# A written-out order of issue replaced by a list scheduler, weights converted in PSUM pieces, and epsilon as a ninth column of a sum

## The chip, the cores and the metric

The kernel runs on one core of one Trainium2 chip. The metric is the device time of one execution in microseconds (us) on that core. Everything is float32 at the borders, except the weights, which arrive as float64 words. The profile shows one execution; its times run from the first to the last instruction (the span).

## The reference

Four batches of four heads attend linearly over 1088 tokens with head size 32; the heads' outputs stand side by side as 128 columns and go through a gated feed-forward layer (here: the ffn) with 1024 inner columns.

```python
def phi(x):
    a = np.einsum('rd,bhsd->bhsr', S1, x)
    b = np.einsum('rd,bhsd->bhsr', S2, x)
    return np.einsum('bhsi,bhsj->bhsij', a, b).reshape(*x.shape[:-1], r * r)
q_p, k_p = (phi(q), phi(k))
kv = np.einsum('bhsf,bhsd->bhfd', k_p, v)
z = np.sum(k_p, axis=2)
num = np.einsum('bhsf,bhfd->bhsd', q_p, kv)
den = np.einsum('bhsf,bhf->bhs', q_p, z)[..., None] + 1e-06
...
h = np.maximum(x @ w_in, 0.0)
for k in range(3):
    conv_out += conv_w[k][None, None, :] * hp[:, k:k + S, :]
gate = 1.0 / (1.0 + np.exp(-conv_out))
return (h * gate @ w_out).astype(np.float32)
```

## The kernel before

**Attention.** Tokens go in chunks of 128, three chunks to a group, three groups to a batch. On the k side of a group, `k_ab` multiplies the chunks with S1 and S2 on TensorE (L389), `k_take` copies the result out of PSUM on ScalarE (L393), `k_phi` makes the outer products (L370, on VectorE or on GpSimd, by the table `KPHI`), and `k_kv` adds them up against v in one bank of PSUM (L425). `k_z`, `k_zmask`, `k_wz` and `k_wq` make the sum z of the batch and fold it with S2 (L405 to L416); `k_kvmask`, `k_kvt` and `k_kvtake` bring the batch's kv into place (L436 to L444). On the q side of a group `q_ab` multiplies (L452), `q_take` copies (L456), `q_ac` and `q_sum` make the denominator (L460, L464), `q_eps` adds epsilon to it (L467, 12 elements a partition), `q_rec` and `q_div` divide (L470, L473), `q_phi` makes the outer products (L370), two `q_t` transpose them (L488), two `q_ttake` copy (L492), `q_x` multiplies with kv (L500), and `q_hi` and `q_lo` split the result x into a rounded part and a rest (L514, L517).

**The ffn.** The tokens of all batches stand in one row of columns, cut into nine segments (382 columns, seven times 510, 404). A unit is one segment with one of eight blocks of 128 inner columns, 72 units in all. A unit is `f_in`, three matmuls in an accumulation (L571 to L573); `f_relu` and `f_mid` on ScalarE (L578, L582); two taps of the convolution on VectorE (L586); `f_gate` on ScalarE (L592); `f_mul` on GpSimd (L597, the last unit's on VectorE); and `f_out`, one float32 matmul into the segment's sum (L602), which the trace shows as two instructions. After eight units the sum is copied and stored (L608, L613). The first segment needs x of one group of tokens only.

**Weights.** A float64 weight becomes a float32 in seven or eight steps: `low` on ScalarE (L289), two bit fields and a clamp on VectorE (L292 to L294), a multiply-add `f` (L295), `power` on ScalarE (L302), `sign` on VectorE (L305), `value` on GpSimd (L311); w_in is split further into a rounded part on ScalarE (L340) and a rest on GpSimd (L343). Each matrix is done in two halves of 512 columns, with all working tiles in SBUF. One packed array of 216 columns (S1, S2, the convolution's weights) goes first, wholly on VectorE.

**Order.** Each engine takes its instructions in program order. Up to a key that stands for the first unit's beginning, the order on four engines is that of keys written out by hand (`FIRST`, `WEIGHTS`); later only the ffn on TensorE and ScalarE is held to such keys, and the rest goes where the framework puts it. Tiles come from pools that rotate; TensorE's results have 4 banks of PSUM for units, 1 for the segment's sum, 3 for the attention. Loads are started on SyncE's queue, and two of them (half of w_in, batch 1's k) on ScalarE's. Eight idle matmuls stand before the first real one, and one more later (L272).

Of the kernel before, what the change touches and what calls it, by code (L numbers as in the profile page):

```python
# [78 lines left out]
STEPS = {
    "k_ab": (0.05, 1.01),  # L80
    "k_take": (0.4, 1),
    "k_phi": (0.65, 1),
    "k_kv": (3.25, 1),
    "k_z": (3.32, 0),
    "k_zmask": (3.47, 0),
    "k_wz": (4.04, 0),
    "k_wq": (4.38, 0),
    "k_kvmask": (5.98, 0),
    "k_kvt": (7.25, 0),
    "k_kvtake": (7.4, 0),  # L90
    "q_ab": (0.2, 0),
    "q_take": (0.4, 0),
    "q_ac": (0.57, 0),
    "q_sum": (0.91, 0),
    "q_eps": (1.28, 0),
    "q_rec": (1.82, 0),
    "q_div": (2.24, 0),
    "q_phi": (3.06, 0),
    "q_t": (5.1, 0),
    "q_ttake": (5.81, 0),  # L100
    "q_x": (6.21, 0),
    "q_hi": (6.4, 0),
    "q_lo": (7.41, 0),
}
# [1 line left out]
FREE = 0.1
# steps of a unit of the ffn after its own key; the last units' products go to VectorE
LATE = 1
LAGS = (0, 0.28, 0.5, 0.6, 0.66, 2.35, 3.5, 5.05, 5.19)
L_IN, L_RELU, L_MID, L_TAPA, L_TAPB, L_GATE, L_MUL, L_OUT, L_STORE = LAGS  # L110
# batch -> (key of its k side, stretch), keys of its groups' q sides
KSIDE = [None, (-2.55, 1.0), (5.56, 1.5), (18.12, 1.78)]
QSIDE = [[None, -2.98, -0.34], [2.08, 8.05, 9.86], [15.15, 31.42, 37.29], [38.03, 45.98, 50.18]]
# the first batch and the weights, on a scale of their own: two steps to a key, the first unit stands at T0
T0 = 18.2
WQ_S = 6.84
FIRST = {
    "k_ab": (7.1, 0.24),
    "k_take": (7.8, 0.48),
# [562 lines left out]
```

## Time and profile before

| | |
|---|---|
| median of 3 runs | 185.1 us (185.1 to 186.12) |
| span of the profiled execution | 183.1 us |
| the profiled execution's own time | not recorded apart from the runs; two of the three took 185.1 us, 2.0 us more than the span |
| TensorE, VectorE, ScalarE, GpSimd busy | 172.1, 153.1, 142.6, 122.8 us |
| mean granted clock of TensorE | 0.972 |
| bytes read, written | 9.15 MB, 2.23 MB |

In the profile PE is TensorE's matmuls, PEld its loads of weights, DVE is VectorE, ACT ScalarE, POOL GpSimd, SP SyncE. The rows of the timeline give start and duration; durations of neighbours on one engine overlap a little, since each starts before the one ahead has drained, so that the cost of one is read from start to start. "x12" after a float32 matmul counts two instructions for each in the program. PEclk is the granted clock of TensorE as a share of the full one.

### The profile page before, as it was taken

The page shows a single profiled execution, that of the slowest core. Times are in us where ns is not written, and L with a number is a line of the kernel's source. Part 1 is how long each engine was busy: PE and PEld are TensorE (multiplying, and loading weights), DVE is VectorE, ACT ScalarE, POOL GpSimd, SP SyncE. Part 2 cuts the span into 40 slices and gives each one's busy share as a digit, 9 for nine tenths or more (in the row PEclk, how much of TensorE's full clock was granted, in tenths as well). Part 3 has the DMA queues.
Part 4 walks back from the last instruction along what each step waited for, and adds up shares of the span by engine and source line. Part 5 has one row for each costly group of instructions (what it writes and reads, how often), then busy time and mean ns, then how long its engine had stood idle before and what let it go on. Part 6 is the DMA issues. An engine that isn't in the chain of part 4 may idle for free.

```text
span 183.1 us, 2698 instructions
## 1 busy us (share of the span) xinstructions
PE 172.1 (94%) x870; PEld 112.9 (62%) x870; DVE 153.1 (84%) x270; ACT 142.6 (78%) x297; POOL 122.8 (67%) x111
## 2 busy tenths in 40 slices
PE   7696888999999999999999999999999999999992
PEld 6584756767777565756666566664656565566640
DVE  2769999997788849977669998898989997999981
ACT  3235455499975798897778999899899999999960
POOL 1135568598985535998556697478569795779760
PEclk9999657999999999999999999999999999999999
DMA  5999992000000100010001001000100100010101
GB/s 141 378 356 343 354 380 53 0 4 2 0 0 4 43 0 2 0 61 0 0 0 57 5 0 57 2 0 0 57 4 0 54 3 0 2 57 0 58 3 45
DMA packets 9005, 11.54 MB, mean 63 GB/s; under 512 B 544, under 2 KB 7712, under 8 KB 8992
## 3 DMA queue, kind: packets, MB, share of 16 engines
q1 hardware_dynamic: 8704, 10.30, 17.1%
q10 hardware_dynamic: 288, 1.08, 1.6%
q8 instruction: 7, 0.11, 0.3%
q14 instruction: 6, 0.05, 0.1%
HBM read 9.15 MB, written 2.23 MB: 62 GB/s over the span
## 4 chain that ended last, share of the span: by engine, by line
PE 57%; POOL 13%; DVE 10%; issue 7%; ACT 4%; DMA 4%; SPq 3%; POOLq 1%; DVEq 0%; ACTq 0%
PE o L602 19%; POOL g L597 13%; PE a L571 7%; PE a L572 6%; PE a L573 6%; DMA w_in_raw<-in_w_in 4%; PE t L425 4%; PE t L500 4%; PE t L452 4%; PE t L488 4%; PE t L389 2%; DVE f L295 2%; ACT s L592 2%; SPq L233 2%; DVE a L586 1%
## 5 line engine op out<-in xcount | busy, mean ns | idle before, releaser
L586 DVE SCALAR_TENSOR_TENSOR a<-h,pws,a 128x510 f32<-128x510 f32 (+2 forms) x144 | 102.4, 722 | 16.8 <-ACT a L582 14.5
L597 POOL TENSOR_TENSOR g<-h,s 128x510 f32<-128x510 f32 (+2 forms) x71 | 86.5, 1223 | 36.5 <-ACT s L592 34.3
L602 PE MATMUL o<-g,w_out_sb 128*128 128x510 f32 (+2 forms) x144 | 70.3, 572 | 0.9 <-DVE o L608 0.5
L578 ACT ACTIVATE h<-a 128x512 f32<-128x512 f32 (+2 forms) x72 | 42.6, 592 | 13.2 <-PE a L573 13.1
L582 ACT ACTIVATE a<-h,pws 128x510 f32<-128x510 f32 (+2 forms) x72 | 49.8, 692 | 0.0
L571 PE MATMUL a<-xhi,whi 128*128 128x512 f32 (+2 forms) x72 | 45.7, 635 | 0.0
L592 ACT ACTIVATE s<-a 128x510 f32<-128x510 f32 (+2 forms) x72 | 42.5, 591 | 3.2 <-DVE a L586 2.8
L602 PEld LDWEIGHTS o<-g,w_out_sb 128*128 128x128 f32 x144 | 26.5, 189 | 8.8 <-POOL g L597 1.8
L572 PE MATMUL a<-xhi,wlo 128*128 128x512 f32 (+2 forms) x72 | 27.9, 388 | 0.0
L573 PE MATMUL a<-xlo,whi 128*128 128x512 f32 (+2 forms) x72 | 27.9, 387 | 0.0
L571 PEld LDWEIGHTS a<-xhi,whi 128*128 128x128 f32 x72 | 13.8, 192 | 13.6 <-issue 7.3
L572 PEld LDWEIGHTS a<-xhi,wlo 128*128 128x128 f32 x72 | 13.8, 192 | 9.3 <-issue 8.7
L370 POOL TENSOR_TENSOR kp<-kab 128x768 f32<-128x768 f32 x9 | 13.8, 1533 | 5.8 <-ACT kab L393 5.7
L573 PEld LDWEIGHTS a<-xlo,whi 128*128 128x128 f32 x72 | 13.7, 190 | 2.5
L370 POOL TENSOR_TENSOR qp<-qm,qab 128x768 f32<-128x768 f32 x9 | 13.6, 1512 | 1.7 <-DVE qm L473 1.5
L389 PEld LDWEIGHTS t<-pws,kt 128*128 128x128 f32 x72 | 10.3, 214 | 6.5 <-issue 3.1
L389 PE MATMUL t<-pws,kt 128*128 128x64 f32 x72 | 11.0, 300 | 1.7 <-DVE m L293 1.4
L452 PEld LDWEIGHTS t<-wq,qt 128*128 128x128 f32 x72 | 10.1, 202 | 3.4 <-issue 1.2
L488 PEld LDWEIGHTS t<-pks,qp 128*128 128x128 f32 x72 | 8.8, 148 | 5.4 <-issue 2.6
L425 PE MATMUL t<-kp,vt 128*64 128x128 f32 x144 | 11.5, 288 | 0.3 <-DMA vt<-in_v 0.3
L488 PE MATMUL t<-pks,qp 128*128 128x128 f32 x72 | 10.9, 288 | 0.8 <-DVE qp L370 0.8
L492 ACT COPY qt<-t 128x384 f32<-128x384 f32 x24 | 10.8, 505 | 1.0 <-PE t L488 0.9
(65 smaller groups left out, 150.5 us busy)
## 6 DMA issues: line engine op xcount, KB each, us to landing
qt<-in_qT SPq DMA_DIRECT2D x4, 544.0 KB, 8.2
vt<-in_v SPq DMA_DIRECT2D x4, 512.0 KB, 9.3
kt<-in_kT SPq DMA_DIRECT2D x3, 544.0 KB, 9.0
w_out_raw<-in_w_out SPq DMA_DIRECT2D x2, 512.0 KB, 8.5
out<-o SPq DMA_DIRECT2D x4, 255.0 KB, 2.2
kt<-in_kT ACTq DMA_DIRECT2D x1, 544.0 KB, 7.5
...
```

The source lines that it names most:

```text
L370: e.tensor_tensor(out=out.rearrange("p c (h i j) -> p (c h) i j", i=R, j=R), in0=a.unsqueeze(3).broadcast_to([P, n, R, R]), in1=b.unsqueez ...
L389: nc.tensor.matmul(pv[:, :, j, :], kt[:, b, c * P : (c + 1) * P], sab, start=True, stop=True)
L488: nc.tensor.transpose(ps[:, j * P : (j + 1) * P], st["qp", g][:, j, P * pr : P * (pr + 1)], ident)
L571: nc.tensor.matmul(a[:, : n + 2], whi[:, w], xhi[:, x], start=True, stop=False)
L572: nc.tensor.matmul(a[:, : n + 2], wlo[:, w], xhi[:, x], start=False, stop=False)
L573: nc.tensor.matmul(a[:, : n + 2], whi[:, w], xlo[:, x], start=False, stop=True)
L578: nc.scalar.activation(h[:, : n + 2], a[:, : n + 2], AF.Relu)
L582: nc.scalar.activation(st["a"][:, :n], h, AF.Copy, scale=cw[:, f, 1:2])
L586: nc.vector.scalar_tensor_tensor(out=a[:, :n], in0=h[:, k : n + k], scalar=cw[:, f, k : k + 1], in1=a[:, :n], op0=ALU.mult, op1=ALU.add)
L592: nc.scalar.activation(s[:, :n], st["a"][:, :n], AF.Sigmoid)
L597: e.tensor_tensor(out=gt[:, :n], in0=st["h"][:, 1 : n + 1], in1=st["s"][:, :n], op=ALU.mult)
L602: nc.tensor.matmul(acc[g][:, :n], w_out_sb[:, f * P : (f + 1) * P], st["g"][:, :n], start=f == 0, stop=f == NF - 1)
```

## The change

All keys and stretches go. A function `graph` lists every step with its engine, an assumed cost, the steps that it needs, and the buffers that it takes and frees; `schedule` runs through them as a list scheduler: of the engines' next possible steps it takes the one that can begin first, and among those of an engine that can begin within 30 ns of each other the one with the lowest due time. It assumes that VectorE and GpSimd exclude each other in steps marked `lock` or `twice`. All four engines follow the resulting order from beginning to end, and every tile stands in the buffer that the scheduler gave it.

Beside the order:

- The weights of w_in and w_out are converted in pieces of 256 columns, eight in all, and the two integer fields stand in a bank of PSUM of the attention's three, not in SBUF. `sign` takes its field from PSUM and writes to a third SBUF tile.
- The packed small weights are split in two arrays, S1 and S2 for the attention (64 columns) and the rest (152 columns), converted one after the other.
- `q_eps` is gone. The tile that `q_ac` writes has a ninth column, set to epsilon once at the start in three buffers, and `q_sum` adds nine elements.
- All loads are on SyncE's queue, in another order; v comes padded with zeros and laid out so that a batch is one transfer (two before, and a memset of the padding), w_out in one row for each partition.
- Of the 24 groups of outer products five change engine: batch 0's third k group and batch 2's third q group go from VectorE to GpSimd, batch 1's first two q groups and batch 3's third k group go from GpSimd to VectorE. VectorE then has seven of them (six before).
- The idle matmuls come from the scheduler: where TensorE's planned gap before 22 us is over 300 ns, one for each 430 ns.

```diff
-CVT = 512
+CVT = 256
-LOADS = "s i0 k0 c v0 q0 i1 v1 o0 o1 q1 k1 k2 v2 q2 q3 k3 v3"
-EARLY = "i0 k1"
-WARM = 8
+    "loads": "s t k0 c v0 i0 q0 o0 o1 k1 i1 v2 k3 v1 q2 k2 v3 q1 q3",
+    "kphi": ["DPP", "PPP", "PPP", "DPD"],
+    "qphi": ["DPP", "DDD", "PPP", "PPP"],
+    "fills": 22000.0,
+POOLS = {"u": 4, "o": 1, "t": 3, "h": 6, "s": 3, "g": 6, "f": 3, "w": 3, "kab": 6, "kp": 4, "qs": 3, "qp": 2, "qt": 4, "kv": 2}
+FILL = 430.0
...
+            if able:
+                soonest = min(t for t, _, _ in able)
+                _, t, _, name = min((key, t, str(name), name) for t, name, key in able if t <= soonest + 30)
+                if best is None or t < best[0]:
+                    best = t, e, name
+        t, e, name = best
+        (_, occ, lat, shared), _, alloc, _ = events[name]
+        for b in alloc:
+            slot[b] = heapq.heappop(pools[kind_of[b]])[1]
+        if e == "PE" and t < cfg["fills"]:
+            fills[name] = max(0, int((t - now[e] - 300) / FILL))
...
+                em = bank(("cv", *key), "t", "em").bitcast(I32)
+                st["e"], st["m"] = em[:, :n], em[:, n : 2 * n]
...
+            if not small:
+                st["w"] = buffer(("w", *key), "w", [P, n], "w", I32)
             nc.vector.scalar_tensor_tensor(
-                out=st["e"], in0=hi, scalar=-(2**31), in1=st["e"], op0=ALU.bitwise_and, op1=ALU.bitwise_or
+                out=st["w"], in0=hi, scalar=-(2**31), in1=st["e"], op0=ALU.bitwise_and, op1=ALU.bitwise_or
             )
...
+        for m in qms:
+            nc.vector.memset(m[:, :, R:], EPS)
...
-        def q_eps(g):
-            nc.vector.tensor_scalar(st["qd", g], st["qd", g], EPS, None, op0=ALU.add)
-
+            nc.vector.reduce_sum(den.rearrange("p g o -> p (g o)"), qms[slot["qs", b, g]], axis=AX.X)
```

**TensorE, from the first real matmul to the first unit.** In the names `t` is a bank of the attention, `a` one of a unit, `kt` and `qt` the loaded k and q (or, with `kv`, the transposed products), `sab`, `pws` and `pts` the small weights. Before, from the beginning on:

```order
L272 MATMUL warm<-idle 128x256 x8
L389 MATMUL t<-pws,kt 128x2x32 x9
L425 MATMUL t<-kp,vt 64x128 x6
L405 MATMUL t<-kab 32x32 x9
L425 MATMUL t<-kp,vt 64x128 x12
L413 MATMUL t<-zt,pws 128x32
L272 MATMUL warm<-idle 128x256
L452 MATMUL t<-wq,qt 128x3x32 x6
L440 MATMUL t<-pks,kvm 128x128
L389 MATMUL t<-pws,kt 128x2x32 x3
L488 MATMUL t<-pks,qp 128x128 x6
```

Now:

```order
L414 MATMUL warm<-idle 128x256 x9
L518 MATMUL t<-sab,kt 128x2x32 x9
L556 MATMUL t<-kp,vt 64x128 x6
L536 MATMUL t<-kab 32x32 x9
L556 MATMUL t<-kp,vt 64x128 x6
L544 MATMUL t<-zt,pts 128x32
L556 MATMUL t<-kp,vt 64x128 x6
L583 MATMUL t<-wq,qt 128x3x32 x3
L571 MATMUL t<-pks,kvm 128x128
L583 MATMUL t<-wq,qt 128x3x32 x6
L414 MATMUL warm<-idle 128x256
L618 MATMUL t<-pks,qp 128x128 x6
```

Nine idle matmuls stand ahead of the first real one where there were eight; the three `q_ab` of batch 0 now all stand before the first transposes.

**VectorE, from the second piece of w_in to the first group's x.** `em` is the pair of integer fields in PSUM. Before, from the second half of w_in on:

```order
L295 SCALAR_TENSOR_TENSOR f<-m,f 128x512
L436 TENSOR_TENSOR kvm<-t,pks 128x128
L460 TENSOR_TENSOR qm<-qab,t 128x96
L464 TENSOR_REDUCE qd<-qm 128x12
L467 TENSOR_SCALAR qd<-qd 128x12
L470 RECIPROCAL qd<-qd 128x12
L460 TENSOR_TENSOR qm<-qab,t 128x96
L473 TENSOR_TENSOR qm<-t,qd 128x96
L464 TENSOR_REDUCE qd<-qm 128x12
L370 TENSOR_TENSOR qp<-qm,t 128x768
L467 TENSOR_SCALAR qd<-qd 128x12
L305 SCALAR_TENSOR_TENSOR e<-w_in_raw,e 128x512
```

Now:

```order
L567 TENSOR_TENSOR kvm<-t,pks 128x128
L443 TENSOR_SCALAR em<-em 128x256
L440 TENSOR_SCALAR em<-w_in_raw 128x256
L446 SCALAR_TENSOR_TENSOR f<-em,f 128x256
L591 TENSOR_TENSOR qm_108<-qab,t 128x12x8
L597 TENSOR_REDUCE qd<-qm_108 128x12
L459 SCALAR_TENSOR_TENSOR w<-w_in_raw,em 128x256
L600 RECIPROCAL qd<-qd 128x12
L604 TENSOR_TENSOR qn<-t,qd 128x96
L591 TENSOR_TENSOR qm_109<-qab,t 128x12x8
L502 TENSOR_TENSOR qp<-qn,t 128x768
```

The additions of epsilon are gone from the chain, one `sign` of 256 columns stands in the middle of it, and the mask of kv stands ahead of the second piece's clamp, no longer behind its multiply-add.

**GpSimd, up to the first products of the ffn.** Before, from batch 0's second q group on:

```order
L370 TENSOR_TENSOR qp<-qm,qab 128x768
L343 TENSOR_TENSOR wlo<-w,whi 128x512
L370 TENSOR_TENSOR kp<-kab 128x768
L311 TENSOR_TENSOR w_out_sb<-e,f 128x512 x2
L597 TENSOR_TENSOR g<-h,s 128x382
L370 TENSOR_TENSOR qp<-qm,qab 128x768
L597 TENSOR_TENSOR g<-h,s 128x382 x3
```

Now:

```order
L502 TENSOR_TENSOR qp<-qn,qab 128x768 x2
L502 TENSOR_TENSOR kp<-kab 128x768 x3
L465 TENSOR_TENSOR w_out_sb<-w,f 128x256
L699 TENSOR_TENSOR g<-h,s 128x382
L465 TENSOR_TENSOR w_out_sb<-w,f 128x256
L699 TENSOR_TENSOR g<-h,s 128x382 x2
```

Five outer products in a row stand ahead of the first product of the ffn.

More of the change, by code (lines that the diff above doesn't have):

```diff
@@ L1 @@
 from contextlib import ExitStack
-from functools import partial
+import collections
+import heapq
 import concourse.bass as bass
@@ L34 @@
 GT = GC * P
+NT = [min(GT, S - g * GT) for g in range(NG)]
 PITCH = S + 1
@@ L79 @@
[L79 to L103, printed above, removed]
-}
@@ L106 @@
[L106 to L119, printed above, removed]
-    "k_phi": (8.3, 0.6),
-    "k_z": (9.4, 0),
-    "k_kv": (8.67, 0.85),
-    "k_zmask": (10.52, 0),
-    "k_wz": (11.04, 0),
-    "k_wq": (11.22, 0),
-    "k_kvmask": (11.6, 0),
-    "k_kvt": (13.14, 0),
-    "k_kvtake": (13.16, 0),
-    "q_ab": (12.0, 0),
-    "q_take": (12.7, 0),
-    "q_ac": (12.9, 0),
-    "q_sum": (13.1, 0),
-    "q_eps": (13.2, 0),
-    "q_rec": (13.3, 0),
-    "q_div": (13.51, 0),
-    "q_phi": (14.53, 0),
-    "q_t": (15.2, 0),
-    "q_ttake": (15.62, 0),
-    "q_x": (17.08, 0),
-    "q_hi": (17.2, 0),
-    "q_lo": (17.6, 0),
-}
@@ L180, in bank, with buffer @@
-    def bank():
-        return ps_t.tile([P, 512], F32, tag="t", name="t")
-    events = []
-    def ev(key, fn, *args, after=(), makes=None):
-        events.append((key, len(events), fn, args, after, makes))
+    banks = ctx.enter_context(tc.tile_pool(name="banks", bufs=1, space=PSUM))
+    def bank(name, kind, what):
+        return banks.tile([P, 512], F32, tag=f"{kind}{slot[name]}", name=what)
+    def buffer(name, kind, shape, what, dtype=F32):
+        return sb.tile(shape, dtype, tag=f"{kind}{slot[name]}", name=what)
@@ L270, in fill @@
+    warm = banks.tile([P, 512], F32, tag="o0", name="warm")
     def fill(n):
@@ L519, in q_lo @@
             )
-        def step(fn, g, *before, pr=None, also=()):
-            name = fn.__name__
-            ev(
-                key(name, 0 if g is None else g),
-                fn,
-                *(() if g is None else (g,) if pr is None else (g, pr)),
-                after=[(b, x) if isinstance(x, str) else (b, *x) for x in before] + list(also),
-                makes=(b, name) if g is None else (b, name, g) if pr is None else (b, name, g, pr),
-            )
-        every = range(NG)
@@ L544, in attention @@
-        chain = (q_ab, q_take, q_ac, q_sum, q_eps, q_rec, q_div, q_phi)
-        for g in every:
-            step(q_ab, g, "k_wq", also=["wqs"])
-            for one, two in zip(chain, chain[1:]):
-                step(two, g, (one.__name__, g))
-            for pr in range(2):
-                step(q_t, g, ("q_phi", g), pr=pr)
-                step(q_ttake, g, ("q_t", g, pr), pr=pr)
-            step(q_x, g, "k_kvtake", ("q_ttake", g, 0), ("q_ttake", g, 1))
-            step(q_hi, g, ("q_x", g))
-            step(q_lo, g, ("q_hi", g))
+        for fn in (k_z, k_zmask, k_wz, k_wq, k_kvmask, k_kvt, k_kvtake):
+            do[fn.__name__, b] = fn
@@ L556, in body @@
+        for g in range(NG):
+            for fn in (k_ab, k_take, k_phi, k_kv, q_ab, q_take, q_ac, q_sum, q_rec, q_div, q_phi, q_x, q_hi, q_lo):
+                do[fn.__name__, b, g] = lambda fn=fn, g=g: fn(g)
+            for fn in (q_t, q_ttake):
+                for pr in range(2):
+                    do[fn.__name__, b, g, pr] = lambda fn=fn, g=g, pr=pr: fn(g, pr)
     for b in range(B):
-        attention(b, partial(attention_key, b))
+        attention(b)
     acc = {}
```

589 lines of the change are left out of this document (360 added, 229 removed).

## Prediction

> **What bounds the kernel now.** I read the busy times first, then the 40 slices.
>
> ```profile
> PE 172.1 (94%) x870; PEld 112.9 (62%) x870; DVE 153.1 (84%) x270; ACT 142.6 (78%) x297; POOL 122.8 (67%) x111
> PE   7696888999999999999999999999999999999992
> PEclk9999657999999999999999999999999999999999
> ```
>
> TensorE is full from the seventh slice to the last but one, and its granted clock falls only in the fifth to seventh. A busy PE can be a waiting one, since its ends are modelled, so the next view is the chain of waits in the middle of the span, and the busy times by stage.
>
> ```profile
> 100.30 0.85 PE o L602 x2
> 101.15 0.23 PE a L571
> ...
> 101.86 0.86 PE o L602 x2
> 20.00:28.00 8.00, 7.49 (x29) 5.67 (x30) 8.00 (x11) 3.67 (x9) 5.61 (x5) 0.50 1.08 354
> 28.00:35.00 7.00, 6.09 (x62) 4.70 (x63) 7.00 (x10) 3.65 (x9) 5.75 (x4) 0.88 0.05 14
> 105.00:120.00 15.00, 15.00 (x62) 9.42 (x61) 13.64 (x25) 14.21 (x30) 11.20 (x9) 1.00 0.05 18
> 165.00:177.00 12.00, 11.52 (x41) 7.33 (x40) 11.48 (x19) 11.24 (x25) 9.56 (x10) 1.00 0.06 23
> ```
>
> The first three rows (and "...") are the chain's, the last four the stages'. The stages' columns are the stretch, its length, then PE, PEld, DVE, ACT and POOL busy, the granted clock, the DMA share and GB/s. A unit of 510 columns takes 1.56 us with nothing between (100.30 to 101.86), 0.71 of it `f_in`: TensorE is at work there, not waiting. So from 35 us on the kernel is a queue of TensorE work, and it ends when that queue does. What can be won is the time before the queue flows: the first unit, the ninth (the first of 512 columns), and how TensorE spends the stage between.
>
> ```profile
> 1.10 6.03 PE L272 MATMUL warm<-idle 128*128 128x256 f32 x16 [1.10 <-POOL idle L265]
> 8.52 2.19 PE L389 MATMUL t<-pws,kt 128*128 128x64 f32 x18 [1.39 <-DVE m L293]
> 14.80 1.47 PE L452 MATMUL t<-wq,qt 128*128 128x96 f32 x12
> 17.61 0.33 PE L440 MATMUL t<-pks,kvm 128*128 128x128 f32 x1 [1.34 <-DVE kvm L436]
> 18.29 0.88 PE L389 MATMUL t<-pws,kt 128*128 128x64 f32 x6 [0.36 <-ACT kv L444]
> 19.93 1.51 PE L488 MATMUL t<-pks,qp 128*128 128x128 f32 x6 [0.76 <-DVE qp L370]
> 27.68 0.67 PE L571 MATMUL a<-xhi,whi 128*128 128x384 f32 x1
> 46.32 0.48 PE L571 MATMUL a<-xhi,whi 128*128 128x512 f32 x1
> 179.61 0.58 DVE L608 COPY o<-o 128x404 f32<-128x404 f32 x1 [1.04 <-PE o L602]
> ```
>
> The first unit starts at 27.68, 19 us after the first real matmul, the ninth at 46.32. In that chain VectorE is the late one, and the next rows say why.
>
> ```profile
> 17.48 0.24 DVE L460 TENSOR_TENSOR qm<-qab,t 128x96 f32<-128x96 f32 x1
> 19.70 1.45 DVE L467 TENSOR_SCALAR qd<-qd 128x12 f32<-128x12 f32 x1
> 23.41 1.74 DVE L294 TENSOR_SCALAR e<-e 128x512 int32<-128x512 int32 x1
> 19.61 1.51 POOL L370 TENSOR_TENSOR kp<-kab 128x768 f32<-128x768 f32 x1 [2.81 <-ACT kab L393]
> 23.35 1.51 POOL L370 TENSOR_TENSOR kp<-kab 128x768 f32<-128x768 f32 x1
> L467 DVE TENSOR_SCALAR qd<-qd x12: 163/679/1451, 18.0 to 143.4; 128x12 f32<-128x12 f32 x12
> L460 DVE TENSOR_TENSOR qm<-qab,t x12: 194/249/255, 17.5 to 141.7; 128x96 f32<-128x96 f32 x12
> L294 DVE TENSOR_SCALAR e<-e x5: 264/415/1741, 6.0 to 28.1; 128x512 int32<-128x512 int32 x4, 128x216 int32<-128x216 int32 x1
> ```
>
> Adding epsilon to 12 elements takes 0.16 us at least and 1.45 at most; the longest ends (21.15) where a GpSimd product ends (21.12). The clamp at 23.41 likewise outlasts the product begun at 23.35. `q_ac`, with an input in PSUM, never exceeds 0.255. So VectorE's work between SBUF tiles waits for GpSimd here, and work that touches PSUM does not.
>
> **The change part by part.** *Epsilon.* Twelve instructions of 0.68 us go (8.2 us of VectorE), twelve reductions get 12 elements more, next to nothing. On the path to the first unit this is worth its 0.2 us for group 0; elsewhere TensorE's queue covers it.
>
> *Conversion in PSUM.* All 40 VectorE steps of the big weights get a PSUM operand and so lose the wait for GpSimd. No row shows such an integer step in PSUM. The bounds are 0.25 us (`q_ac`, 96 columns) and 0.75 us (a tap of 510 columns); I take 0.43, near the 384-column `q_lo` (0.55, below) less its third. Then the first two pieces take 10 x 0.43 = 4.3 us where the halves took much longer; at 0.75 they would take 3.2 us more, of which half lies on the path.
> [...]
>
> *Start.* The loads are now in one queue, S1 and S2 first and k of batch 0 third: 64 + 152 + 544 KB.
>
> ```profile
> 2.00:3.00 1.00, 1.00 (x4) 0.73 (x4) 0.13 (x1) 0.99 (x2) 0.00 (x0) 1.00 0.78 164
> 3.00:4.00 1.00, 1.00 (x4) 0.82 (x3) 0.00 (x0) 0.14 (x1) 0.00 (x0) 1.00 0.93 262
> 4.00:5.00 1.00, 1.00 (x4) 0.82 (x3) 0.00 (x0) 0.00 (x0) 0.00 (x0) 1.00 0.96 326
> L370 POOL TENSOR_TENSOR kp<-kab 128x768 f32<-128x768 f32 x9 | 13.8, 1533 | 5.8 <-ACT kab L393 5.7
> L492 ACT COPY qt<-t 128x384 f32<-128x384 f32 x24 | 10.8, 505 | 1.0 <-PE t L488 0.9
> L517 DVE TENSOR_TENSOR xlo<-t,xhi 128x384 fp32r<-128x384 f32 x8 | 4.4, 549 | 0.1
> L597 POOL TENSOR_TENSOR g<-h,s 128x382 f32<-128x382 f32 x8 | 8.0, 999 | 2.4 <-ACT s L592 2.3
> L586 DVE SCALAR_TENSOR_TENSOR a<-h,pws,a 128x382 f32<-128x382 f32 x16 | 9.6, 606 | 1.4 <-ACT a L582 1.2
> 45.29 0.61 PE t L389 x6
> 47.91 0.64 PE t L452 x6
> 56.90 0.81 PE t L425 x12
> ```
>
> At these rates 0.76 MB has landed by 5.2 us. But nine idle matmuls stand ahead of the first `k_ab`, and eight took 6.03 us, 16 instructions of 0.4 us for most of it, though the clock column says 1.00. The scheduler counts 0.43 us each, the trace 0.75. So the ninth ends near 7.1 + 0.4 = 7.5, and **`k_ab` starts at 7.6, not 5.2**: 0.9 us earlier than 8.52, the rest of the early load is lost.
> Thence by the rows: three `k_ab` 2.0; the last two outer products now follow each other on GpSimd (9.5 + 2 x 1.5 = 12.5; one of them was VectorE's); `k_kv` 0.8 and a `q_ab` until 14.0. Two ScalarE copies, kv's first, both shorter than the 0.505 of L492, bring `q_ac` to 14.95, where it was 17.48: 2.5 us won, because VectorE is no longer stuck. `q_ac` to the transposes took 2.45 (17.48 to 19.93); less epsilon, plus a `sign` ahead of it, the same: 17.4. Transposes 0.65, copies to 18.9, `q_x` 0.8 to 19.75, `q_hi` 0.5 (as L492's copy of the same width), `q_lo` 0.55, and the second and third `k_ab` of batch 1 end at 20.9. **First unit at 21.0**, 6.7 us earlier; much of that is that TensorE had half its clock there before.
>
> *From the first to the ninth unit.* GpSimd sets this stage. From 18.0, when its next `q_div` is there, it has five outer products (7.5 us), then four `value` steps (0.7 each, in proportion to the 0.999 of 382 columns) between four units' products: 18.0 + 7.5 + 4 x 0.7 + 4 x 1.0 = 32.3. TensorE's order has the fourth `f_out` ahead of units five to eight: 32.3 + 0.7 + four `f_in` of 0.55 (three quarters of 0.71) + two `k_ab` and a `q_ab` 1.86 = 37.1. VectorE has 16 taps, 24 conversion steps, two more `q_lo` and two masks there, start to start some 0.1 less than their durations: 8.3 + 7.9 + 0.9 + 0.3 = 17.4 from 20.4 on, 37.8, when the eighth unit's taps are done. **Ninth unit at 37.2**, 9.1 us before 46.32. By then one `k_ab` and one `f_out` more (0.6 + 0.65) and a pair of transposes less (0.65) are done: another 0.6.
>
> *After that* TensorE has the same work, since no matmul is added or dropped but one idle one, and the order alternates `f_out` and `f_in` as before, six `f_out` left after the last `f_in` in both. I cost it at nothing: 46.32 to 183.1 is 136.8 us, and stays. The five changes of engine add one outer product to VectorE and take one off GpSimd; in 105 to 120 these have 1.4 and 3.8 us free, so TensorE covers it.
>
> Sum: 37.2 + 136.8 - 0.6 = 173.4 us of span, 9.7 less than 183.1. The median of the runs shown is 2.0 above the span: 185.1 - 9.7 = 175.4, which I round to **175.5 us**.
>
> **Rivals.** *The plan holds from the start (171 us).* If the idle matmuls cost what the scheduler counts, `k_ab` starts at 5.4 and all behind moves 2.2 us; a better packed middle might give 2 more. For it: the load is there. Against: 0.4 us for each of 16 instructions.
>
> *The clock falls (179.5 us).* Before, TensorE worked 1.2 us (0.33 + 0.88) between 16.3 and 19.9, and the clock went to 0.50 for 10 us (the stages above). Now I count 2.5 us of work between 15.6 and 19.0, not much denser. At half clock from 18 on, the 11 us of work up to the ninth unit would take 5 more, less 1 of slack: +4.
> [...]
>
> *The order holds an engine up (187 us, slower).* Before, half the engines were free to take what was ready; now each waits for its next instruction in a plan made with assumed costs. The place is ScalarE after the ninth unit: in 105 to 120 it has 0.8 us in 15 free. If its fixed order makes it wait for VectorE or GpSimd over 5% of the time, it replaces TensorE as the bound, and at 13% the 136 us become 148: 175.5 + 11.5. For it: the assumed costs differ from the trace (`k_kv` 0.65 against 0.81, the idle matmuls). Against: ScalarE's order was fixed before too, with the same four banks.
>
> *It does not do what it says (185 us).* The early units may only wait longer for w_in's second half, whose load now stands behind w_out and k of batch 1, so that units five to eight come no sooner. Against: by the load rates it lands near 16 us.
>
> **How the numbers follow.** The forecast gets 0.55 (172.5 to 178), the plan holding 0.17, the clock 0.20, the hold-up 0.04, no effect 0.04. The range takes in the rivals at 171 and 179.5 and the 1.6 us of PSUM cost: 169.5 to 181. A measurement of this kernel tells 1% from no change; faster by over 1%: 0.92, within: 0.04, slower: 0.04.
>
> **What would show it.** Right: 18 idle instructions until 7.5 with `k_ab` waiting for TensorE alone; no conversion step on w_in above 0.5 us; the first unit near 21 and the ninth near 37; granted clock 1.00 from 21 on. Wrong: a clock of 0.50 in 18 to 28, a ninth unit after 40, or PE below 14.5 of 15 us in the stages from 45 to 150.

## The result, and the profile after

The changed kernel takes 179.89 us in the median of four runs (178.78 to 180.51), 0.9697 of the time before, with a 95% interval of 0.9648 to 0.9745. The forecast was 175.5 us (169.5 to 181): of the 9.7 us that it expected, 5.2 came. The profiled execution took 179.29 us with a span of 177.1. Where a ratio and a median below don't fit each other (the run with five idle matmuls), the ratio leaves out the two of its executions that took over 1.5% longer than its fastest.

The page of the changed kernel, busy times first, then the 40 slices:

```profile
PE 168.1 (95%) x872; PEld 109.2 (62%) x872; DVE 147.1 (83%) x288; ACT 145.6 (82%) x308; POOL 121.2 (68%) x116
PE   7997789998999999999999999999999999999992
PEclk9999999999999999999999999999999999999999
```

The dip of the clock in the fifth to seventh slice is gone, and from the seventh slice on TensorE's digits are nines, but for the tenth and the last. The same in stages (columns as in the prediction: stretch, length, then PE, PEld, DVE, ACT, POOL busy, granted clock, DMA share, GB/s):

```profile
16.00:21.00 5.00, 3.92 (x24) 2.53 (x24) 4.36 (x16) 3.10 (x11) 3.85 (x4) 1.00 1.02 415
21.00:28.00 7.00, 5.92 (x63) 4.99 (x65) 6.19 (x17) 4.40 (x13) 5.70 (x5) 1.00 0.86 344
...
35.00:45.00 10.00, 9.14 (x56) 7.21 (x55) 8.51 (x21) 8.27 (x23) 8.00 (x9) 1.00 0.00 1
...
105.00:120.00 15.00, 15.00 (x62) 9.27 (x61) 13.68 (x26) 14.13 (x28) 10.78 (x10) 1.00 0.05 17
```

In 21 to 28 TensorE now runs 63 instructions, where 20 to 28 held 29. It is idle for 1.08 us in each of the first two stages and for 0.86 in the third, and not again until the last units. The marks that the prediction named, in the timeline of TensorE:

```profile
1.10 6.45 PE L414 MATMUL warm<-idle 128*128 128x256 f32 x18 [1.10 <-POOL idle L397]
7.38 2.12 PE L518 MATMUL t<-sab,kt 128*128 128x64 f32 x18
...
13.58 0.88 PE L583 MATMUL t<-wq,qt 128*128 128x96 f32 x6 [0.40 <-issue]
...
17.88 0.52 PE L618 MATMUL t<-pks,qp 128*128 128x128 f32 x3 [0.28 <-DVE qp L502]
...
19.85 0.87 PE L628 MATMUL t<-qt,kv 128*64 128x384 f32 x4
...
22.35 0.88 PE L518 MATMUL t<-sab,kt 128*128 128x64 f32 x6 [0.41 <-ACT kab L522]
23.04 0.42 PE L673 MATMUL a<-xhi,whi 128*128 128x384 f32 x1
...
42.05 0.50 PE L673 MATMUL a<-xhi,whi 128*128 128x512 f32 x1 [0.86 <-ACT s L694]
```

Up to the first transposes (17.88, where 17.4 was predicted) the chain keeps within 0.5 us of the prediction. Then it falls behind: `q_x`, which was to end at 19.75, only starts at 19.85, the first unit comes at 23.04 (21.0 was predicted) and the ninth at 42.05 (37.2). From the ninth to the end of the span it is 135.05 us (136.2 predicted). The question of the experiments is what stands between 17.88 and 42.05.

### The profile page after: what moved, and what is told of

Same layout as the page of the kernel before. It is cut to its first block, busy times and chain, and to the rows that moved or that the text cites. A ratio compares the mean times of both kernels' runs of the same rounds, so it can differ in the third digit from the quotient of the medians.

```text
span 177.1 us, 2740 instructions
## 1 busy us (share of the span) xinstructions
PE 168.1 (95%) x872; PEld 109.2 (62%) x872; DVE 147.1 (83%) x288; ACT 145.6 (82%) x308; POOL 121.2 (68%) x116
## 4 chain that ended last, share of the span: by engine, by line
PE 83%; DVE 5%; POOL 4%; ACT 4%; issue 1%; POOLq 1%; ACTq 0%
PE o L704 33%; PE a L673 10%; PE a L674 8%; PE a L675 8%; PE t L556 5%; PE t L628 4%; PE t L618 4%; PE warm L414 4%; PE t L583 3%; POOL kp L502 3%; PE t L518 2%; POOL qp L502 1%; PE t L536 1%; ACT em L454 1%; ACT a L684 1%
## 5 line engine op out<-in xcount | busy, mean ns | idle before, releaser
L688 DVE SCALAR_TENSOR_TENSOR a<-h,pts,a 128x510 f32<-128x510 f32 (+2 forms) x144 | 102.6, 724 | 12.7 <-ACT a L684 9.9
L684 ACT ACTIVATE a<-h,pts 128x510 f32<-128x510 f32 (+2 forms) x72 | 49.3, 686 | 0.9
L673 PE MATMUL a<-xhi,whi 128*128 128x512 f32 (+2 forms) x72 | 46.6, 648 | 0.9 <-ACT s L694 0.9
L704 PEld LDWEIGHTS o<-g,w_out_sb 128*128 128x128 f32 x144 | 25.2, 189 | 10.7 <-POOL g L699 4.7
L622 ACT COPY qt<-t 128x384 f32<-128x384 f32 x24 | 11.8, 498 | 0.8 <-PE t L618 0.8
L502 POOL TENSOR_TENSOR qp<-qn,qab 128x768 f32<-128x768 f32 x8 | 12.0, 1514 | 0.4 <-DVE qn L604 0.4
L556 PE MATMUL t<-kp,vt 128*64 128x128 f32 x144 | 10.5, 281 | 0.7 <-POOL kp L502 0.6
L583 PE MATMUL t<-wq,qt 128*128 128x96 f32 x72 | 10.0, 277 | 1.2 <-issue 0.4
L583 PEld LDWEIGHTS t<-wq,qt 128*128 128x128 f32 x72 | 9.2, 191 | 3.1 <-issue 1.1
L518 PEld LDWEIGHTS t<-sab,kt 128*128 128x128 f32 x72 | 9.2, 191 | 2.9 <-ACT kab L522 1.6
```

The source lines that it names most:

```text
L502: e.tensor_tensor(out=out.rearrange("p c (h i j) -> p (c h) i j", i=R, j=R), in0=a.unsqueeze(3).broadcast_to([P, n, R, R]), in1=b.unsqueez ...
L583: nc.tensor.matmul(pv[:, :, j, :], qt[:, b, c * P : (c + 1) * P], wq[:, b], start=True, stop=True)
L673: nc.tensor.matmul(a[:, : n + 2], whi[:, w], xhi[:, x], start=True, stop=False)
L684: nc.scalar.activation(st["a"][:, :n], h, AF.Copy, scale=cw[:, f, 1:2])
L688: nc.vector.scalar_tensor_tensor(out=a[:, :n], in0=h[:, k : n + k], scalar=cw[:, f, k : k + 1], in1=a[:, :n], op0=ALU.mult, op1=ALU.add)
L704: nc.tensor.matmul(acc[g][:, :n], w_out_sb[:, f * P : (f + 1) * P], st["g"][:, :n], start=f == 0, stop=f == NF - 1)
```

## Experiments

In all runs the kernel before took 185.1 to 185.3 us in the median; ratios are to it. "After" is the changed kernel.

### Which part brings the gain

**Epsilon alone**, put into the kernel before:

```diff
-            nc.vector.tensor_tensor(out=m, in0=heads(st["qab", g][:, 0]), in1=heads(st["qps", g][:, 2]), op=ALU.mult)
+            nc.vector.tensor_tensor(out=m[:, :, :R], in0=heads(st["qab", g][:, 0]), in1=heads(st["qps", g][:, 2]), op=ALU.mult)
...
-        def q_eps(g):
-            nc.vector.tensor_scalar(st["qd", g], st["qd", g], EPS, None, op0=ALU.add)
```

> The kernel before with only the ninth column of the sum in place of the addition of epsilon. The prediction's step: VectorE loses 8 us of work that lies beside TensorE's queue, the path to the first unit 0.2 us; 184.5 to 185.1. Rival: the 1.45 us addition at 19.70 stood ahead of the sign step of w_in's second half and of later steps, and what it frees moves the first units up by 1 us or more: 183.5 to 184.

Measured: 183.98 us, ratio 0.9938 (0.9924 to 0.9953). The first unit starts at 27.43 for 27.68, so the chain to it gains 0.25 us, as predicted; the ninth unit starts at 46.20 for 46.32, the first segment's sum is copied at 59.16 for 59.84 and the last at 178.58 for 179.61. So epsilon is worth 1.1 us and not 0.2: the time is the rival's, but not by the rival's path, since some 0.9 of it is won behind the ninth unit, where the prediction had it covered. Which of the later additions carries it was not isolated.

**PSUM alone**, for w_in alone, in the kernel before:

```diff
+                if psum and t != "f":
+                    st[t] = ps_u.tile([P, 512], F32, tag="a", name="a").bitcast(I32)
+                else:
+                    st[t] = cv.tile([P, n], d, tag=t, name=t)
```

> The kernel before with one edit: the two integer fields of w_in stand in two of the units' PSUM banks, which are idle until the first unit; order, halves of 512 columns, engines and w_out stay. Theory A (GpSimd's products stop VectorE's steps between SBUF tiles, and PSUM alone takes the stop away in any order): no clamp of w_in above 0.75 us, where 1.74 stood, the first unit 1.3 to 1.8 us earlier than 27.68, time 183.3 to 184. Rival B (the stage before the first unit is set by TensorE at half clock, 7.49 of 8 us busy in 20 to 28, and VectorE's stall is hidden behind it): the clamp falls just the same, but the first unit stays within 0.5 us of 27.68 and the time at 184.7 to 185.5; then the PSUM fields pay only together with the new order.

Measured: 183.94 us, ratio 0.9918 (0.9898 to 0.9939). VectorE's timeline on w_in's second half (first field, clamp, multiply-add), in the kernel before and in this run:

```profile
13.65 1.33 DVE L292 TENSOR_SCALAR e<-w_in_raw 128x512 int32<-128x512 int32 x1 [0.30 <-DMA w_in_raw<-in_w_in]
...
15.24 0.41 DVE L294 TENSOR_SCALAR e<-e 128x512 int32<-128x512 int32 x1
15.58 1.77 DVE L295 SCALAR_TENSOR_TENSOR f<-m,f 128x512 f32<-128x512 int32 x1
```

```profile
13.70 0.69 DVE L296 TENSOR_SCALAR a<-w_in_raw 128x512 int32<-128x512 int32 x1 [0.30 <-DMA w_in_raw<-in_w_in]
...
14.90 0.69 DVE L298 TENSOR_SCALAR a<-a 128x512 int32<-128x512 int32 x1
15.50 0.68 DVE L299 SCALAR_TENSOR_TENSOR f<-a,f 128x512 f32<-128x512 int32 x1
```

The first field and the multiply-add, which stood beside GpSimd's work on the first half (`value`, 1.27 us at 13.43, and the rest, 1.36 us at 15.44, in before), fall from 1.33 and 1.77 us to 0.69 and 0.68. The clamp, which stood alone, rises from 0.41 to 0.69: that is the price of the PSUM operand. (The 1.74 us that the expectation names is a clamp on w_out, which stays in SBUF and takes 1.73 here too.) `q_ac` comes 1.2 us earlier (16.29 for 17.48), the first unit as much (26.50), and the time is 1.3 us less: theory A in the main. Four executions with mean clocks of 0.972, 0.969, 0.991 and 0.991 took 183.89 to 183.97, so in the old order the clock made no difference that shows (where these executions differ in their starts isn't on record).

**All but PSUM**: after, with the two fields in two SBUF tiles again, its order untouched:

```diff
-                em = bank(("cv", *key), "t", "em").bitcast(I32)
-                st["e"], st["m"] = em[:, :n], em[:, n : 2 * n]
+                st["e"] = buffer(("cv", *key), "ce", [P, n], "ce", I32)
+                st["m"] = buffer(("cv", *key), "cm", [P, n], "cm", I32)
```

> The changed kernel, in its own order, with the two integer fields of each piece in two SBUF tiles instead of the two halves of one PSUM bank; some small buffers are shared to make room. Theory 1 (shared bank): in the changed kernel ScalarE's power step waits for the other field's step (4.1 us in all) and VectorE's multiply-add waits for the power step (2.8 us), only because both fields stand in one bank; with two tiles both waits go below 1 us, the ninth unit comes near 39.5 instead of 42.05, and the time falls to about 177.5. Theory 2 (GpSimd's hold on SBUF): field steps between SBUF tiles wait for GpSimd again, their mean rises from 0.43 us to 0.8 or more, the ninth unit stays at 42 or comes later, and the time is 180 to 183.

Measured: 186.27 us, ratio 1.006 (1.004 to 1.008), slower than before. The clamp's line in this run (count, least, median and most ns; then who waited for it, us and times), TensorE's two marks, and the clamp's line in after:

```profile
L443 DVE TENSOR_SCALAR ce<-ce x8: 377/1101/1605, 11.2 to 42.3; 128x256 int32<-128x256 int32 x8
...
  ACT ce L454: 8.0, 6
```

```profile
25.18 0.67 PE L673 MATMUL a<-xhi,whi 128*128 128x384 f32 x1
...
46.78 0.79 PE L673 MATMUL a<-xhi,whi 128*128 128x512 f32 x1 [2.00 <-ACT s L694]
```

```profile
L443 DVE TENSOR_SCALAR em<-em x8: 421/429/433, 11.3 to 38.0; 128x256 int32<-128x256 int32 x8
```

In PSUM the eight clamps take 0.42 to 0.43 us, all alike; in SBUF 0.38 to 1.61, and ScalarE waits 8.0 us in all for them; the first unit comes at 25.18, and the ninth at 46.78. This is theory 2, and worse than its 180 to 183: the granted clock reads 0.62 in 21 to 28 and 0.89 in 45 to 60, where after's reads 1.00, and no run here tells what of the loss is the clock's and what the stretched steps'. (The small buffers that this run shares weren't tried apart either.)

So the change without the PSUM fields is worth less than nothing, PSUM for w_in alone in the old order 1.3 us, and PSUM for both matrices in the new order 6.4 (186.27 to 179.89), the clock's part included. In this order, fixed on all engines, a stretched step is handed on to whoever stands behind it: it pays only when its steps take the time that the plan gave them.

### The start

**Five idle matmuls** ahead of the first `k_ab` in place of nine:

```diff
-            fills[name] = max(0, int((t - now[e] - 300) / FILL))
+            fills[name] = min(5, max(0, int((t - now[e] - 300) / FILL)))
```

> The changed kernel with five idle matmuls ahead of the first real one instead of nine, nothing else. By the prediction's step on the idle matmuls the first k_ab starts at 5.7 (when k has landed) instead of 7.38 and the first and ninth unit move about 1.7 us ahead: time 178. Rival a: TensorE then runs k_ab at half its clock (4 us instead of 2.1), and nothing is won: 179.5 to 180. Rival b: the chain is held by the first piece of w_in, which landed at 10.8, not by k_ab: the k side comes earlier but the first unit stays near 23, 179.5.

**w_in's first load earlier**, the order of the engines untouched:

```diff
-    for name in CFG["loads"].split():
+    for name in "s t k0 i0 c v0 q0 o0 o1 k1 i1 v2 k3 v1 q2 k2 v3 q1 q3".split():
```

> The changed kernel with the order of the loads alone changed: the first 512 columns of w_in (1 MB) go ahead of conv and of v of batch 0; the order on the four engines stays. Theory A (VectorE waits 1.4 us for w_in in the order's place, with z and q_ac of the first chain behind it): w_in's fields start 1.4 to 2.3 us earlier, q_ab by about 0.9 us, first unit 22.0 to 22.4, time 178.7 to 179.3. Rival B (v of batch 0 then comes late and k_kv, which needs it, takes the place of the wait): k_kv waits for the DMA by 0.5 us or more, first unit 23 or later, time 179.6 to 181.

Five idle matmuls: 180.95 us (178.45 to 182.14), ratio 0.9682 (0.9638 to 0.9726). `k_ab` starts at 5.82, 1.56 us earlier, but the first `q_ab` at 13.29, only 0.29 earlier:

```profile
10.58 0.43 DVE L437 TENSOR_SCALAR em<-w_in_raw 128x256 int32<-128x256 int32 x1 [2.57 <-DMA w_in_raw<-in_w_in]
10.92 0.17 DVE L540 TENSOR_TENSOR zt<-t,pks 32x32 f32<-32x32 f32 x1
...
13.29 0.88 PE L583 MATMUL t<-wq,qt 128*128 128x96 f32 x6 [0.94 <-ACT wq L547]
```

VectorE stands 2.57 us in front of a step that waits for w_in, and `zt`, which the chain needs, is the next in its order. TensorE then waits 0.94 us more for `wq`, a copy that stands behind `power` in ScalarE's order, while `power` waits 0.77 for the second field. The first unit comes at 23.74 (rival b, in the main), and the clock reads 0.67 in 16 to 21. The early load of k is lost to the fixed orders, not to the idle matmuls alone.

w_in earlier: 179.91 us, ratio 0.9707 (0.9683 to 0.9732), and neither theory holds. The wait for w_in is gone, but `zt` then waits 0.89 us for `k_z`, which is no sooner: in this execution `k_ab` starts at 7.97, since the same nine idle matmuls took 7.04 us instead of 6.45. From `k_ab` to `q_ab` it is 6.16 us (6.20 in after). Which of the two binds depends on the execution: in after `k_z` ends at 11.17 and `zt` starts at 11.21, behind w_in's first step, so both come together; in the last run below, where the nine took 5.55 us, TensorE waits 0.55 us for a `zt` that w_in holds up.

### The clock

**More idle matmuls before**, eight of them in the gaps ahead of the stage at half clock:

```diff
-FILL = [(11.45, 1)]
+FILL = [(11.45, 1), (13.1, 5), (15.19, 3)]
```

> The kernel before with eight idle matmuls more on TensorE, five ahead of k_kvt and three ahead of the first q_t of batch 0, where it stood idle for 1.34 and 0.76 us before its clock went to 0.50; later instructions that have no fixed place may change places a little. Theory A (the half clock in 20 to 28 costs TensorE some 4 us, and most of what the change won is that this loss is gone): granted clock 0.95 or more in 21 to 28, the first unit 2 us or more before 27.68, time 181.5 to 183. Rival B (VectorE, busy 7.00 of 7 in that stage, sets the first unit, and a slow clock only stretches matmuls that would wait for VectorE otherwise; the run with w_in's fields in PSUM took 183.94 whether its mean clock was 0.972 or 0.991): the clock rises, the first unit moves less than 0.7 us, time 184.6 to 185.6.

Measured: 186.87 us, ratio 1.008 (1.0056 to 1.0105). The clock rose to 0.90 in 21 to 28 and fell to 0.61 in 28 to 35 instead (0.88 before), and the first unit came at 30.33, 2.65 us later. The free instructions had changed places: `q_x` stood at 22.85 before, and now waits for a `q_div` (it writes `qm`) that stands behind a w_out step which GpSimd holds up (it waits 1.02 us for `value`, then takes 1.72 beside GpSimd's outer product of 1.51 at 24.41, where the one at 20.31 takes 0.42). So the run gives no size for the clock. It does show TensorE waiting 2.62 us for VectorE in a stage whose clock reads 0.90:

```profile
24.48 1.72 DVE L292 TENSOR_SCALAR e<-w_out_raw 128x512 int32<-128x512 int32 x1 [1.02 <-POOL w L311]
...
26.42 1.40 PE L500 MATMUL t<-qt,kv 128*64 128x384 f32 x4 [2.62 <-DVE qm L473]
```

**One idle matmul fewer** in after, the one at 16.98 ahead of the transposes:

```diff
-    "fills": 22000.0,
+    "fills": 14000.0,
```

> The changed kernel without the one idle matmul that stands ahead of the first transposes (16.98, 0.62 us with the wait); nothing else changes. Theory A (that matmul keeps the clock up, and the clock is what the change won): the clock falls to 0.5 or 0.7 somewhere in 16 to 28, time 181 to 183. Rival B (the matmuls around it are enough, or the clock is of little worth here): time 179.5 to 180.5, mean clock 0.985 or above.

Measured: 180.71 us (179.95 to 181.84), ratio 0.9735 (0.9687 to 0.9783). Of four executions two had a mean clock of 0.968 and took 181.84 and 181.43, two had 1.000 and took 179.95 and 179.99. The profiled one is of the first kind (its stages, then two marks of TensorE):

```profile
16.00:21.00 5.00, 3.98 (x21) 2.67 (x20) 4.37 (x15) 2.52 (x7) 4.10 (x5) 0.72 1.02 416
21.00:28.00 7.00, 6.59 (x39) 5.54 (x37) 4.47 (x11) 3.49 (x9) 5.15 (x4) 0.50 0.86 346
...
12.94 0.88 PE L583 MATMUL t<-wq,qt 128*128 128x96 f32 x6 [0.36 <-issue]
...
44.59 0.50 PE L673 MATMUL a<-xhi,whi 128*128 128x512 f32 x1 [0.85 <-ACT s L694]
```

The executions with a fallen clock took 1.4 to 1.9 us longer than the others. But an execution's start moves too (see the last section), and the profiled one started early. From its first `q_ab` (12.94) to the ninth unit (44.59) it took 31.65 us, where after took 28.47 with the clock at 1.00: in the stage itself the fall costs 3.2 us, not far from the 4 of the prediction's rival. After's own four runs spread in this way too: 0.998 and 0.997 with 179.29 and 178.78, twice 0.988 with 180.5. None of the twelve executions with the matmul in this order (after, w_in earlier, and the small products below) fell under 0.988, so it seems to keep the clock up, as far as so few show. In the profiled execution TensorE's longest gap between the first matmul and 21 us is 0.74 us, ahead of the transposes at 17.25, and the clock reads 0.72 in 16 to 21 and 0.50 in 21 to 28; what makes it fall is not shown.

### From the first to the ninth unit

**The scheduler told of the waits**: it now counts on `power` after `m`, on `f` after `power` and on `sign` after `f`:

```diff
-            ev((w, j, "power"), c_act(n), [(w, j, "clamp")], uses=[b], key=key)
+            ev((w, j, "power"), c_act(n), [(w, j, "m")], uses=[b], key=key)
```

> The changed kernel with the scheduler told of the waits that the shared bank makes (the second field after the clamp, power after the second field, multiply-add after power), so that the order of issue is computed again; every step stays as it is. Theory 1: the stalls cost because the plan did not know them; ScalarE's wait for the second field falls from 4.1 us to 1.5 or less, the ninth unit comes 1 to 2 us earlier, 178.5. Theory 3 (the banks are short, whoever knows): the ninth unit stays at 41.5 to 43 and the time at 179.5 to 181.

Measured: 179.78 us (179.42 to 180.0), ratio 0.9707 (0.9688 to 0.9727): the same as after. ScalarE's wait for the second field falls from 4.1 to 2.0 us, but the whole order is another one (first unit at 24.74, ninth at 46.39), so neither theory's marks can be read. A plan that knows of the waits won nothing.

**The units' banks for the early pieces**, one for both fields, then two:

```diff
-            ev((w, j, "e"), c_dve(n), [d], [(b, "t")], key=key)
+            kind = "u" if (w, j) in EARLY else "t"
+            ev((w, j, "e"), c_dve(n), [d], [(b, kind)], key=key)
```

> The changed kernel with one edit: the field pair of the first three pieces (both of w_in's first half, the first of w_out) takes a bank of the units' four, idle then, and not one of the attention's three; the scheduler then makes its order anew. Theory A (the pieces hold banks that the attention's matmuls need, seen as waits of 0.41 at 22.35 and 0.28 at 18.68): those two waits go, first unit 22.2 to 22.6 where it was 23.04, time 179.0 to 179.5. Rival B (the late w_in, whose first 256 columns land near 10.8 us, and VectorE's own queue set the first unit): first unit within 0.3 us of 23.04, time 179.6 to 180.3.

> As the run with one unit bank, but the two fields of these three pieces stand in two banks, so that power no longer waits for the step that writes the other field. Theory A (the shared bank ties the two fields together: power on ScalarE waits 1.01, 0.76 and 0.94 us in order, ahead of relu and mid of the first units, and what is behind it there is late): these waits fall under 0.3 each for the pieces moved, the ninth unit comes 1.0 to 2.0 us before 42.05, time 178 to 179. Rival B (TensorE has other matmuls to do while ScalarE waits, so the units' work is only put in another order): the waits fall, the ninth unit moves less than 0.5 us against the run with one bank, and the time stays within 0.5 us of it.

Measured: 180.89 us (0.9756, 0.9728 to 0.9784) and 180.21 (0.9714, 0.9681 to 0.9748). The first unit came earlier, at 22.09 and 22.50, and the time did not follow. The scheduler had made a whole new order: in the first run four units now follow each other at 22.1 to 24.1, and then TensorE waits twice:

```profile
25.38 1.53 PE L560 MATMUL t<-kp,vt 128*64 128x128 f32 x24 [0.94 <-DVE f L450]
...
28.68 0.91 PE L708 MATMUL o<-g,w_out_sb 128*128 128x382 f32 x2 [1.77 <-POOL g L703]
```

A first unit that starts sooner is no gain if what it needs next is not there. Both runs changed the order along with the banks, so against after they don't tell what the banks are worth; against each other the ninth unit stands still (42.43 and 42.42), though the second run's first `q_ab` came 1.06 us later.

**GpSimd relieved**: batch 1's three outer products of the k side are cut to 64 of 768 columns, which `k_kv` reads in place of the rest:

```diff
+            if b == 1:
+                outer(nc.gpsimd, kp, heads(ab[:, 0]), heads(ab[:, 1]), 1)
```

> The changed kernel, order as it is, with batch 1's three outer products of the k side cut to a twelfth on GpSimd (64 of 768 columns; k_kv reads these in place of the rest, so batch 1's kv is another one): GpSimd's block of 4.46 us at 21.56 falls to about 0.8. Theory A (GpSimd's work sets the stage from the first to the ninth unit, as the prediction has it): the ninth unit 2.5 to 3.5 us before 42.05, time 176.5 to 177.5. Rival B (VectorE's and ScalarE's fixed orders with their waits for each other set it): the ninth unit less than 1.2 us earlier, time 178.8 to 180.

Measured: 179.30 us (178.72 to 179.48), ratio 0.9667 (0.9640 to 0.9695). The timeline of this run (GpSimd and TensorE), and of after (VectorE's `sign` of w_out's second piece with them):

```profile
21.70 0.29 POOL L501 TENSOR_TENSOR kp<-kab 128x64 f32<-128x64 f32 x1
...
26.50 0.88 PE L557 MATMUL t<-kp,vt 128*64 128x128 f32 x12 [0.62 <-issue]
...
28.40 1.01 POOL L701 TENSOR_TENSOR g<-h,s 128x382 f32<-128x382 f32 x1 [3.29 <-ACT s L696]
...
42.23 0.50 PE L675 MATMUL a<-xhi,whi 128*128 128x512 f32 x1 [0.86 <-ACT s L696]
```

```profile
21.56 4.46 POOL L502 TENSOR_TENSOR kp<-kab 128x768 f32<-128x768 f32 x3
...
25.84 0.41 DVE L459 SCALAR_TENSOR_TENSOR w<-w_out_raw,em 128x256 int32<-128x256 int32 x1
...
26.35 0.88 PE L556 MATMUL t<-kp,vt 128*64 128x128 f32 x12 [0.62 <-POOL kp L502]
...
28.25 1.00 POOL L699 TENSOR_TENSOR g<-h,s 128x382 f32<-128x382 f32 x1 [1.55 <-ACT s L694]
...
31.36 0.99 POOL L699 TENSOR_TENSOR g<-h,s 128x382 f32<-128x382 f32 x1 [0.47 <-ACT s L694]
...
34.08 0.73 POOL L465 TENSOR_TENSOR w<-w,f 128x256 f32<-128x256 f32 x1 [1.02 <-DVE w L459]
34.77 1.00 POOL L699 TENSOR_TENSOR g<-h,s 128x382 f32<-128x382 f32 x1
```

Over 3.5 us of GpSimd's work are gone, and nothing comes earlier: `k_kv` starts at 26.50, the ffn's first product at 28.40, the ninth unit at 42.23, all 0.15 to 0.18 us later than in after, as is the first `q_ab` (0.14). From the first `q_ab` (13.72 here, 13.58 in after) to the ninth unit it is 28.51 us and 28.47. **GpSimd does not set this stage**: relieved, it only waits longer for ScalarE's gate (3.29 us for 1.55). After's profile puts `k_kv`'s 0.62 us of waiting down to GpSimd's `kp`; with `kp` done early it waits just as long. The buffers that the scheduler gave out name a better cause: `k_kv` of batch 1 takes the bank that the second piece of w_out holds until its `sign`, which ends at 26.25, 0.10 ahead of `k_kv`; in the run with small products `sign` ends 0.11 ahead of it too.

**The second field in a bank of its own**, for the first five pieces, in the bank of the segment's sum, which holds nothing but idle matmuls' results until the first `f_out`; the order on all engines is after's:

```diff
+HALF = {("i", 0): (0, 0), ("i", 1): (0, 1), ("o", 0): (1, 0), ("i", 2): (1, 1), ("o", 1): (1, 0)}
...
+                if key in HALF:
+                    t, h = HALF[key]
+                    if t not in spare:
+                        spare[t] = banks.tile([P, 512], F32, tag="o0", name="ms")
+                    st["m"] = spare[t].bitcast(I32)[:, h * n : (h + 1) * n]
```

> The changed kernel, its order on all four engines as it is; the second field m of the first five pieces stands in the segment sum's bank of PSUM, which is idle until the first f_out, so that power no longer waits for m, f no longer for power, and m no longer for the clamp. Theory A (from the first to the ninth unit VectorE and ScalarE wait for each other in the fixed order, and these waits carry the delay): power's waits of 1.01 and 0.76 us at 23.31 and 25.10 fall by 0.4 each, f's four waits of 0.49 go, the first unit comes near 22.5, the ninth 0.8 to 1.5 us before 42.05, time 178.2 to 179.2. Rival B (TensorE's own order sets the stage, with matmuls enough between the units' ones, so VectorE and ScalarE only finish earlier): the waits fall, the ninth unit moves less than 0.4 us, time 179.4 to 180.5.

Measured: **177.46 us (176.55 to 177.97, six runs), ratio 0.9575 (0.9546 to 0.9603)**, faster than both kernels. ScalarE's waits (what it waited for: us in total, times, longest) and its timeline, first in after:

```profile
ACT em L454 <- DVE em L440: 4.1, 5, 1.0
```

```profile
12.32 0.37 ACT L454 ACTIVATE em<-em 128x256 int32<-128x256 int32 x1 [0.76 <-DVE em L440]
12.60 0.19 ACT L547 COPY wq<-t 128x32 f32<-128x32 f32 x1
...
23.31 0.37 ACT L454 ACTIVATE em<-em 128x256 int32<-128x256 int32 x1 [1.01 <-DVE em L440]
```

and in this run, with TensorE's marks:

```profile
ACT em L462 <- DVE em L451: 0.9, 3, 0.4
ACT em L462 <- DVE em L448: 0.8, 1, 0.8
```

```profile
12.04 0.37 ACT L462 ACTIVATE em<-em 128x256 int32<-128x256 int32 x1 [0.31 <-DVE em L451]
...
21.63 0.37 ACT L462 ACTIVATE em<-em 128x256 int32<-128x256 int32 x1 [0.36 <-DVE em L451]
...
22.01 0.42 PE L681 MATMUL a<-xhi,whi 128*128 128x384 f32 x1
...
23.21 0.38 ACT L462 ACTIVATE em<-em 128x256 int32<-128x256 int32 x1
...
24.63 0.88 PE L564 MATMUL t<-kp,vt 128*64 128x128 f32 x12
...
40.15 0.50 PE L681 MATMUL a<-xhi,whi 128*128 128x512 f32 x1 [0.83 <-ACT s L702]
```

`power` (L454, here L462) waited for `m` (L440), which it doesn't read, because both fields lay in one bank (and in one tile of the program; no run puts two tiles in one bank); `f` waited for `power` in turn (2.8 us in after, 1.1 here). With the fields apart ScalarE's 4.1 us of waiting become 0.9 behind the clamp and 0.8 behind the `m` of a piece that wasn't moved, `k_kv` waits no longer, and the ninth unit comes 1.90 us earlier. Of these 1.54 lie behind the first `q_ab`: from it to the ninth unit it is 26.93 us for 28.47. The other 0.36 lie ahead of it (13.22 for 13.58), and they are no luck of the start: TensorE's idle matmuls ended 0.9 us earlier here, but w_in's first step came 0.18 later (11.05 for 10.87), and `q_ab` follows the copy `wq`, which stands behind `power` on ScalarE; `power` waited 0.76 us there in after and 0.31 here. Theory A, and more than it forecast; whether the bank or the tile ties the fields together is not shown.

## Why the prediction was right and wrong

- **That the start of TensorE's queue is what can be won: right.** TensorE works without a gap in the stages from 45 to 150 (15.00 of 15 us busy in each), before and after, and what is gained there stays gained: the ninth unit to the end takes 135.05 us (136.2 predicted).
- **`k_ab` at 7.6: right** (7.38), and for its reason, nine idle matmuls of 6.45 us.
- **0.43 us for a conversion step in PSUM: right**, 0.42 to 0.43 for the clamp. That the clamp is no longer stretched is shown by the run with SBUF fields (0.38 to 1.61 there); that it is GpSimd that stretches it is read from before, where the addition of epsilon begun at 19.70 ends at 21.15 and GpSimd's product at 21.12, and from w_in alone, where the steps beside GpSimd's work fall to 0.69 and 0.68. The worth in this order, 6.4 us with what the clock adds, is more than the whole gain. The PSUM operand has a price: the second field takes 0.28 us in SBUF (median of that run) and 0.43 in PSUM, and the clamp of 512 columns 0.41 and 0.69 (w_in alone).
- **`q_ac` at 14.95, transposes at 17.4: right** within 0.5 us (15.18, 17.88). **`q_x` until 19.75: 0.9 us late**, since it starts at 19.85 and takes 0.8: the second three transposes wait (0.28 us at 18.68) for a bank that a `q_div` holds, so that the six take 1.2 us where 0.65 was counted.
- **First unit at 21.0: wrong by 2.0.** The step that failed is "the second and third `k_ab` of batch 1 end at 20.9": they start at 21.06 and 22.35, each behind `k_take`, 0.34 and 0.41 us, with banks short and ScalarE's order holding `power` ahead of its copies. With `m` apart the unit starts at 22.01, so half of the 2.0 is the shared bank's; the other half was not isolated.
- **"GpSimd sets this stage": wrong.** The step that failed is the sum to 32.3, which counts GpSimd's work and puts its waits at nothing. The work was sized rightly (five products, four `value` steps and four products of the ffn, 14.3 us by sum and by trace), but the fourth product ends at 35.77, because GpSimd stands 3.0 us in this stretch, 1.55 and 0.47 for ScalarE's gate and 1.02 for VectorE's `sign`. With less work it only waits longer. The runs put VectorE and ScalarE in its place, which wait for each other over the shared bank: the prediction read the fields' new place as the end of a wait and missed that the same bank starts another. Ninth unit: 42.05 for 37.2 (past 40, which the prediction named as a sign that it is wrong); of these 4.85 us 2.0 come from the first unit and 2.8 from this stage. 1.9 of the whole is shown to be the shared bank, the rest is not split further.
- **Epsilon 0.2 us: too low**; alone it brings 1.1, some 0.9 of it behind the ninth unit. The changed kernel wins 1.15 there that the prediction didn't count; that this is epsilon's is likely, but not shown in its order.
- **The rival "the clock falls", 179.5 us: its number came true, in the main not by its mechanism.** The clock reads 1.00 in every stage of after's profiled execution (179.29) up to 165, and 0.98 in 165 to 177. In two of its four executions the mean was 0.988, and these took 180.5, so a smaller fall has its part in the median. Where the clock fell to 0.50 (the run with one idle matmul fewer), the stage took 3.2 us longer; the rival's 4 was about right as a price.
- **"The order holds an engine up" after the ninth unit: no**, ScalarE's fixed order shows no loss there. It did hold engines up, but ahead of it.
- **The sum:** 4.85 late at the ninth unit, 1.15 won behind it, 0.2 more around the span and 0.6 from the profiled execution to the median make 4.5 us, from the unrounded 175.4 to 179.9. The 1.15 that no term foresaw offsets a part of the delay: without this luck the error would be larger.

## What to carry to other kernels

Before an order is fixed on all engines, make each step's time independent of its neighbours; else, as in the run with SBUF fields (clamps of 0.38 to 1.61 us, 186.27 us for 179.89), the plan passes the stretches on. When intermediates move into PSUM, try fields that different engines touch in different banks: here the bank (and tile) that two fields shared came with 4.1 us of waiting on ScalarE that neither the data nor the scheduler's list shows, and 1.7 were left when most pieces had their fields apart. And take the name that a profile gives to a wait as a guess where the instruction waits for several things; cut the named work, and see whether the wait goes (`k_kv`'s 0.62 us stayed).

## What the runs showed of the chip beside this

- The same nine idle matmuls at the start took 5.55 us in one profiled execution (the fields apart) and 7.08 in another (two unit banks), with seven others between, while the granted clock's digit is 9 in both from the first slice on. So `k_ab` moves by up to 1.5 us (6.48 to 8.00) between executions with the same start. What follows moves less where it waits for w_in (with the fields apart `k_ab` starts 0.90 us before after's and the first `q_ab` 0.36, with five idle matmuls 1.56 and 0.29), and a mark is better compared by its distance from the one before.
- The first 512 columns of w_in, sixth in the same order of loads, were there for VectorE between 9.61 us (the run with one unit bank) and 11.16 (with two).
- A lower mean clock is not always a longer time: the run with w_in in PSUM took 183.9 us at 0.969 and at 0.991.
